# Far token tiles transposed on VectorE from a copy in DRAM, with three orders changed around the attention stage

## The chip, the core and the metric

The kernel runs on one core of a Trainium2 chip. Five engines work side by side, each through its own queue in order: PE (TensorE, matrix products; its weight loads are listed as PEld), DVE (VectorE), ACT (ScalarE), POOL (GpSimd) and SP (SyncE, which here only issues DMA transfers). The metric is the device time of one execution in microseconds (us). Shown are the median of three runs and one further execution that was profiled.

## The reference, cut to what matters

One transformer block over 2048 tokens of width 1024, in float32:

```python
h   = x + A(layernorm(x), wqkv, w_phi, wo)
out = h + relu(layernorm(h) @ w1) @ w2

def A(x, wqkv, w_phi, wo):                     # 32 heads of 32
    q, k, v = heads(x @ wqkv)
    pq, pk = q @ w_phi, k @ w_phi              # a 32x32 matrix for each head
    phi(p) = concat(softmax(p), softmax(-p))
    kv, z = phi(pk).T @ v, sum over tokens of phi(pk)
    o = (phi(pq) @ kv) / (phi(pq) . z + 1e-6)
    return merge(o) @ wo
```

## The kernel before, in words

**Products.** A product is split into three matmuls (`mm3`, lines 182 to 184): an operand is held as a rounded high half and the remaining low half, and high x high, high x low and low x high are summed. ACT makes the high half (a copy), DVE or POOL the low half (a subtraction).

**Steps.** The program is a list of items in a fixed order, and an item is a run of steps; a step is one `mm3` of one weight unit (128x512). In the first part an item is eight steps: one tile of 128 tokens against eight weight units. Items 0 to 31 are keys and values (four column quarters s of eight tiles) for tiles 0 to 7, called near; items 32 to 47 are queries (two halves) for the same tiles; items 48 to 79 and 80 to 95 are the same for tiles 8 to 15, called far. So far tiles are first used at step 384. Output weights follow at item 96, then the two feed-forward products. `when(step, f)` hangs a helper call behind a step; helpers are issued to the engines' queues in that order. What a helper issues runs as early as its data and its queue allow.

**Weight units.** `Units.advance` is called behind every step. It loads raw weight blocks into six buffers and splits them into a ring of ten units: ACT writes the high half (line 125), POOL or DVE the low half (line 129). A group of eight units serves all eight tiles of a quarter, so most of the next eight become writable only while the last item of a quarter runs, one each step, and each is wanted nine steps later. Such a place is called a switch here. Switches lie at steps 64, 128, 192, ... 448, 512 and so on.

**Far tiles.** A near or far tile of x is normalized and turned so that features lie on partitions. For far tiles, `ln_load` and `ln_stats` first read x for its mean and variance (key "s", from step 80 on, 16 steps apart), and `ln_power` (three short POOL instructions, lines 231 to 233) makes the scale. Later x is loaded a second time, normalized on ACT (line 239), transposed by eight PE transposes (`ln_turn`, line 246) into two PSUM banks, and split from there: ACT two copies of 128x512 (line 178), DVE two subtractions of 128x512 (line 179). That is done between steps 321 and 387, tile by tile, eight steps apart.

**Other work of POOL in that stretch.** `t_sum` (line 363, four subtractions of 128x256 at a time) prepares feed-forward weights: a 512 KB load, four subtractions, a 512 KB store, with two buffers in turn. `kv_z` (line 454) adds up key features, `q_fourth` (line 544) makes short products.

**Attention.** Far queries and attention overlap. For each of 32 units u: `at_sums` (POOL, line 595), `at_reduce` (DVE, line 602), `at_cross` (ACT, four 32x32 copies, line 613), `at_den` (POOL, 617 and 618), `at_inverse` (DVE, 621), `at_scale` (POOL, 631), `at_turn` (DVE, a transpose in 32x32 blocks, line 637), and for each pair of units `at_num` (PE, line 650, 32 small matmuls, 16 of each unit) and `at_low` (DVE, 667). Query items need `q_first` (DVE, lines 516 to 521) and `q_third` (DVE, 534 and 535). Six of the output-weight units live in buffers of their own, named `wf`, in a pool opened by `to_far`.

## Time and profile before

| quantity | value |
|---|---|
| median of three runs | 1872.97 us (1872.37 to 1873.45) |
| profiled execution, its own time | 1870.48 us |
| its span, first to last instruction | 1868.7 us |
| mean granted TensorE clock | 0.999 |
| PE busy | 1856.5 us, 99% of the span |
| DVE, ACT, POOL busy | 1063.8, 770.5, 979.0 us |

The span is the time from the first to the last instruction; the execution's own time has 1.8 us more around it. The chain of waits is followed back from the last instruction: at each point it names the work or the wait that was last to end. A timeline row gives start, duration, engine, line, operation and, in brackets, how long the engine sat idle before it and what ended that. Numbers of steps stand nowhere in the trace; they come from the code, by counting the matmuls of line 182, one for each step.

### The profile page before, as it was taken

The page shows a single profiled execution, that of the slowest core. Times are in us where ns is not written, and L with a number is a line of the kernel's source. Part 1 is how long each engine was busy: PE and PEld are TensorE (multiplying, and loading weights), DVE is VectorE, ACT ScalarE, POOL GpSimd, SP SyncE. Part 2 cuts the span into 40 slices and gives each one's busy share as a digit, 9 for nine tenths or more (in the row PEclk, how much of TensorE's full clock was granted, in tenths as well). Part 3 has the DMA queues.
Part 4 walks back from the last instruction along what each step waited for, and adds up shares of the span by engine and source line. Part 5 has one row for each costly group of instructions (what it writes and reads, how often), then busy time and mean ns, then how long its engine had stood idle before and what let it go on. Part 6 is the DMA issues. An engine that isn't in the chain of part 4 may idle for free.

```text
span 1868.7 us, 28840 instructions
## 1 busy us (share of the span) xinstructions
PE 1856.5 (99%) x10064; PEld 1516.3 (81%) x10064; DVE 1063.8 (57%) x1655; ACT 770.5 (41%) x1379; POOL 979.0 (52%) x991
## 2 busy tenths in 40 slices
PE   9999999999999999999999999999999999999999
PEld 7777788888887777888888888888888888888887
DVE  7787678677689878575555653443433333343333
ACT  5322245233333333354455554444444444444442
POOL 4887745888947988343333222222344444444443
PEclk9999999999999999999999999999999999999999
DMA  7988798666575676887888975666677677777765
GB/s 229 286 294 288 231 289 270 190 203 202 178 227 181 223 243 203 280 278 232 247 262 259 324 249 184 193 201 205 225 223 215 216 218 239 238 215 217 216 216 177
DMA packets 333635, 433.04 MB, mean 232 GB/s; under 512 B 28720, under 2 KB 194608, under 8 KB 333488
## 3 DMA queue, kind: packets, MB, share of 16 engines
q1 hardware_dynamic: 299696, 414.41, 70.1%
q10 hardware_dynamic: 33792, 16.78, 3.2%
q8 instruction: 79, 1.29, 0.3%
q14 instruction: 68, 0.56, 0.1%
HBM read 293.21 MB, written 137.89 MB: 231 GB/s over the span
## 4 chain that ended last, share of the span: by engine, by line
PE 93%; DVE 3%; POOL 1%; issue 1%; ACT 0%; DMA 0%; SPq 0%; ACTq 0%; DVEq 0%; POOLq 0%
PE mm L182 24%; PE mm L183 24%; PE mm L184 24%; PE ac L182 4%; PE ac L184 4%; PE ac L183 4%; PE tp L184 2%; PE tp L183 2%; PE tp L182 2%; PE tp L246 1%; PE ac L465 1%; PE ac L650 1%; DVE qsm L534 0%; DVE qe L637 0%; POOL w L129 0%
## 5 line engine op out<-in xcount | busy, mean ns | idle before, releaser
L129 POOL TENSOR_TENSOR w<-raw,w 128x512 fp32r<-128x512 f32 x353 | 469.0, 1331 | 698.3 <-ACT w L125 663.2
L125 ACT ACTIVATE w<-raw 128x512 fp32r<-128x512 f32 x686 | 409.4, 626 | 508.8 <-PE mm L184 232.4
L129 DVE TENSOR_TENSOR w<-raw,w 128x512 fp32r<-128x512 f32 x333 | 271.0, 815 | 511.6 <-ACT w L125 507.6
L182 PE MATMUL mm<-w,xT 128*128 128x512 f32 x768 | 306.0, 398 | 0.0
L183 PE MATMUL mm<-w,xT 128*128 128x512 f32 x768 | 300.2, 391 | 0.4 <-POOL w L401 0.4
L184 PE MATMUL mm<-w,xT 128*128 128x512 f32 x768 | 299.6, 390 | 0.0
L182 PE MATMUL mm<-hT,w 128*128 128x512 f32 x672 | 261.5, 389 | 0.0
L183 PE MATMUL mm<-hT,w 128*128 128x512 f32 x672 | 261.5, 389 | 0.0
L184 PE MATMUL mm<-hT,w 128*128 128x512 f32 x672 | 261.5, 389 | 0.0
L182 PEld LDWEIGHTS mm<-w,xT 128*128 128x128 f32 x768 | 144.4, 188 | 35.2 <-issue 4.1
L184 PEld LDWEIGHTS mm<-w,xT 128*128 128x128 f32 x768 | 144.4, 188 | 30.9
L363 POOL TENSOR_TENSOR b<-b 128x256 f32<-128x256 f32 x176 | 143.6, 816 | 48.0 <-DMA b<-in_w_dram 38.6
L183 PEld LDWEIGHTS mm<-w,xT 128*128 128x128 f32 x768 | 144.6, 188 | 29.2 <-POOL w L401 1.0
L184 PE MATMUL mm<-w 128*128 128x512 f32 x392 | 152.6, 389 | 0.0
L182 PE MATMUL mm<-w 128*128 128x512 f32 x392 | 152.6, 389 | 0.0
L183 PE MATMUL mm<-w 128*128 128x512 f32 x392 | 152.6, 389 | 0.0
L182 PEld LDWEIGHTS mm<-hT,w 128*128 128x128 f32 x672 | 126.2, 188 | 26.4
L183 PEld LDWEIGHTS mm<-hT,w 128*128 128x128 f32 x672 | 126.2, 188 | 26.2
L184 PEld LDWEIGHTS mm<-hT,w 128*128 128x128 f32 x672 | 126.2, 188 | 26.0
L183 PEld LDWEIGHTS mm<-w 128*128 128x128 f32 x392 | 73.6, 188 | 15.3
L184 PEld LDWEIGHTS mm<-w 128*128 128x128 f32 x392 | 73.6, 188 | 15.2
L182 PEld LDWEIGHTS mm<-w 128*128 128x128 f32 x392 | 73.6, 188 | 15.3
(173 smaller groups left out, 3106.0 us busy)
## 6 DMA issues: line engine op xcount, KB each, us to landing
raw<-t SPq DMA_DIRECT2D x224, 256.0 KB, 3.9
raw<-ad SPq DMA_DIRECT2D x196, 256.0 KB, 3.0
raw<-in_w_dram SPq DMA_DIRECT2D x168, 256.0 KB, 3.1
ad<-c SPq DMA_DIRECT2D x112, 256.0 KB, 3.6
b<-in_w_dram SPq DMA_DIRECT2D x44, 512.0 KB, 5.8
t<-b SPq DMA_DIRECT2D x44, 512.0 KB, 5.0
ad<-s SPq DMA_DIRECT2D x84, 256.0 KB, 4.1
ed<-qe ACTq DMA_DIRECT2D x64, 256.0 KB, 4.1
```

The costliest lines, as they stand in the source:

```text
L125: nc.scalar.activation(w[:, 0, :], raw[1], AF.Copy)
L129: eng.tensor_tensor(out=w[:, 1, :], in0=raw[1], in1=w[:, 0, :].bitcast(F32), op=ALU.subtract)
L182: pe.matmul(ps, a_hi, b_hi, start=first, stop=False, skip_group_check=more)
L183: pe.matmul(ps, a_hi, b_lo, start=False, stop=False, skip_group_check=more)
L184: pe.matmul(ps, a_lo, b_hi, start=False, stop=last, skip_group_check=more)
L246: pe.transpose(pt[:, k, :], xn[:, (4 * j + k) * P:(4 * j + k + 1) * P], ident)
L363: pool.tensor_tensor(out=tsum[*u, *out], in0=tsum[*u, *a], in1=tsum[*u, *b], op=ALU.subtract)
L465: pe.matmul(kv_ps[s][g][32 * i:32 * (i + 1), 0:64], vt[:, 32 * h:32 * (h + 1)], phi[:, 64 * h:64 * (h + 1)], start=first, stop=last)
L650: pe.matmul(banks[g][32 * c:32 * (c + 1), 256 * j:256 * (j + 1)], kvL[rows, 2 * q + h // 4, 32 * (h % 4):32 * (h % 4 + 1)], phT_of[u - 1 + ...
```

## The change

**Far tiles.** For tiles 8 to 15, x is read once. Behind its statistics (`early` is now 80 + 26 for each tile) `far_norm` normalizes it on ACT into a second buffer, with features regrouped; `far_keep` stores that buffer to a DRAM tile `xm`, so laid out that tokens and feature groups are exchanged between rows and columns; `far_back` loads it again from step 300 on, 11 steps apart; `far_turn` transposes it in 32x32 blocks on DVE, in place; `far_high` copies the high half on ACT and `far_low` subtracts on POOL, both over 128x1024 elements read with a step of 256 elements innermost. The PE transposes of far tiles, their PSUM copies and subtractions, and the second load of x are gone. The values are the same as before.

**Turn seven.** `at_turn` of unit 7 is issued five steps sooner. **Crossing copies.** For units 8 and up `at_cross` is issued two steps later and `at_den` one step later. **Output-weight buffers.** The pool of `wf` buffers is opened two items sooner, in `to_wo`; three of its six are usable from there and the others from `to_far` on.

```diff
+    xm = {t: dram.tile([P, D], F32, name=f"xm{t}") for t in range(HT, NT)}
...
     def ln_load(key, parts):
-        xin[key] = xlp.tile([P, D], F32, name="xl") if key[0] == "x" and key[1] >= HT and key[1] % 4 > 1 else \
-            lnp.tile([P, D], F32, name="xin")
+        xin[key] = lnp.tile([P, D], F32, name="xin")
...
+    def far_norm(t):
+        sc, src = xst.pop(("s", t)), xin.pop(("s", t))
+        xin["m", t] = y = lnp.tile([P, D], F32, name="xin")
+        act.activation(y.rearrange("p (a c k) -> p c a k", a=4, c=NK), src.rearrange("p (c a k) -> p c a k", a=4, c=NK),
+                       AF.Identity, bias=sc[:, 1:2], scale=sc[:, 0:1])
+
+    def far_keep(t):
+        sp.dma_start(xm[t].rearrange("(a t) (g x) -> (t g) a x", a=4, g=4),
+                     xin.pop(("m", t)).rearrange("p (a x) -> p a x", a=4))
+
+    def far_back(t):
+        xnt["x", t] = y = xlp.tile([P, D], F32, name="xl") if t % 4 > 1 else fp_ln.tile([P, D], F32, name="xn")
+        sp.dma_start(y, xm[t])
+
+    def far_turn(t):
+        v.transpose(xnt["x", t], xnt["x", t])
+
+    def far_view(y):
+        return y.rearrange("p (g c t) -> p c t g", g=4, c=NK)
+
+    def far_high(t):
+        act.activation(xT[t][:, 0].rearrange("p c (t g) -> p c t g", g=4), far_view(xnt["x", t]), AF.Copy)
+
+    def far_low(t):
+        lo, hi = (xT[t][:, s].rearrange("p c (t g) -> p c t g", g=4) for s in (1, 0))
+        pool.tensor_tensor(out=lo, in0=far_view(xnt.pop(("x", t))), in1=f32(hi), op=ALU.subtract)
...
-            early = 80 + 16 * (t - HT)
+            early, late_ = 80 + 26 * (t - HT), 330 + 11 * (t - HT)
             when(early, ln_load, ("s", t), x_part(t))
-            when(early + 18, ln_stats, ("s", t))
-            when(early + 18, xin.pop, ("s", t))
-            when(early + 22, ln_power, ("s", t))
-            load_ = turn - 88 + 8 * (t - HT) if t < HT + 4 else turn - 36
-            stages = (load_, None, None, turn - 8, turn + 1, turn + 1)
+            when(early + 12, ln_stats, ("s", t))
+            when(early + 16, ln_power, ("s", t))
+            when(early + 20, far_norm, t)
+            when(early + 23, far_keep, t)
+            when(late_ - 30, far_back, t)
+            do(n, 0, x_open, t)
+            for step, f in ((0, far_turn), (4, far_high), (7, far_low)):
+                when(late_ + step, f, t)
+            continue
...
+        far = wos.enter_context(tc.tile_pool(name="wofar", bufs=6, side="right", reuse_waits="tile"))
+        for _ in range(3):
+            far.tile([P, 2, 512], F32R, name="wf")
+        W.far = Ring(far, 3, [P, 2, 512], F32R, "wf")
 
     def to_far():
-        far = wos.enter_context(tc.tile_pool(name="wofar", bufs=6, side="right", reuse_waits="tile"))
-        W.far = Ring(far, 6, [P, 2, 512], F32R, "wf")
+        W.far.bufs = 6
...
-                               (14, at_cross), (16, at_den), (18, at_inverse), (20, at_scale), (26, at_turn)):
+                               (14 if u < 8 else 16, at_cross), (16 if u < 8 else 17, at_den), (18, at_inverse),
+                               (20, at_scale), (21 if u == 7 else 26, at_turn)):
```

Three places show how the orders moved. Line numbers past line 199 are higher in the changed kernel. The first is POOL's queue from the switch at step 384 on. `w<-raw,w` is a weight split, `smq` is `q_fourth`, `b` is a part of `t_sum`, `zacc` is `kv_z`. Before:

```order
L129 TENSOR_TENSOR w<-raw,w 128x512 x2
L544 TENSOR_TENSOR smq<-qsm 128x16 x2
L129 TENSOR_TENSOR w<-raw,w 128x512
L544 TENSOR_TENSOR smq<-qsm 128x16 x2
L129 TENSOR_TENSOR w<-raw,w 128x512
L363 TENSOR_TENSOR b<-b 128x256
L544 TENSOR_TENSOR smq<-qsm 128x16 x2
L363 TENSOR_TENSOR b<-b 128x256 x3
L454 TENSOR_TENSOR zacc_360<-zacc_360,kphi 128x512
```

The same stretch of POOL's queue now, where `xT<-xn,xT` and `xT<-xl,xT` are `far_low`:

```order
L129 TENSOR_TENSOR w<-raw,w 128x512 x2
L571 TENSOR_TENSOR smq<-qsm 128x16 x2
L129 TENSOR_TENSOR w<-raw,w 128x512
L281 TENSOR_TENSOR xT<-xn,xT 128x1024
L571 TENSOR_TENSOR smq<-qsm 128x16 x2
L129 TENSOR_TENSOR w<-raw,w 128x512
L281 TENSOR_TENSOR xT<-xn,xT 128x1024
L390 TENSOR_TENSOR b<-b 128x256
L571 TENSOR_TENSOR smq<-qsm 128x16 x2
L390 TENSOR_TENSOR b<-b 128x256 x3
L481 TENSOR_TENSOR zacc_368<-zacc_368,kphi 128x512
L281 TENSOR_TENSOR xT<-xl,xT 128x1024
```

Three of the eight subtractions of `far_low` (tiles 12, 13 and 14) now stand between the splits and sums of this stretch; tile 15's follows a few rows later.

The second place is DVE's queue around unit 7 of attention; `qe<-qe` under STREAM_TRANSPOSE is `at_turn`, `qmx` and `qe<-mm,qmx` are `q_first`, `qtz` is `at_reduce`, `qden` is `at_inverse`. Before:

```order
L602 TENSOR_REDUCE qtz<-ez 128x16
L516 TENSOR_REDUCE qmx<-mm 128x16
L517 TENSOR_REDUCE qmx<-mm 128x16
L520 TENSOR_TENSOR qe<-mm,qmx 128x4x128
L521 TENSOR_TENSOR qe<-qmx,mm 128x4x128
L602 TENSOR_REDUCE qtz<-ez 128x16
L534 TENSOR_REDUCE qsm<-qe 128x4x2x4
L535 RECIPROCAL qsm<-qsm 128x32
L637 STREAM_TRANSPOSE qe<-qe 128x1024
L621 RECIPROCAL qden<-qden 128x32
```

The same stretch of DVE's queue now:

```order
L629 TENSOR_REDUCE qtz<-ez 128x16
L664 STREAM_TRANSPOSE qe<-qe 128x1024
L543 TENSOR_REDUCE qmx<-mm 128x16
L544 TENSOR_REDUCE qmx<-mm 128x16
L547 TENSOR_TENSOR qe<-mm,qmx 128x4x128
L548 TENSOR_TENSOR qe<-qmx,mm 128x4x128
L629 TENSOR_REDUCE qtz<-ez 128x16
L561 TENSOR_REDUCE qsm<-qe 128x4x2x4
L562 RECIPROCAL qsm<-qsm 128x32
L648 RECIPROCAL qden<-qden 128x32
```

The transpose of unit 7 has moved ahead of a `q_first`, a `q_third` and the second `at_reduce` of unit 8; nothing else in this stretch has moved.

The third place is ACT's queue at the output-weight units; `qden<-qtz` is `at_cross`, `oT<-ac` the copy behind `at_num`. Before:

```order
L125 ACTIVATE wf<-raw 128x512
L613 ACTIVATE qden<-qtz 32x32 x4
L125 ACTIVATE wf<-raw 128x512 x2
L613 ACTIVATE qden<-qtz 32x32 x4
L125 ACTIVATE wf<-raw 128x512 x3
```

The same stretch of ACT's queue now:

```order
L125 ACTIVATE wf<-raw 128x512 x2
L640 ACTIVATE qden<-qtz 32x32 x4
L125 ACTIVATE wf<-raw 128x512 x3
L640 ACTIVATE qden<-qtz 32x32 x4
L125 ACTIVATE wf<-raw 128x512
```

Of the six copies for `wf` units, two now stand ahead of the first crossing copies and five ahead of the second, where one and three stood before.

4 lines of the change are left out of this document (2 added, 2 removed).

## The prediction

> **What bounds the kernel now.** I read the page's first part and its chain of waits first, then the waits of PE, then the timeline at each place where PE stood or nearly stood. The share of busy time:
>
> ```profile
> PE 1856.5 (99%) x10064; PEld 1516.3 (81%) x10064; DVE 1063.8 (57%) x1655; ACT 770.5 (41%) x1379; POOL 979.0 (52%) x991
> PE 93%; DVE 3%; POOL 1%; issue 1%; ACT 0%; DMA 0%; SPq 0%; ACTq 0%; DVEq 0%; POOLq 0%
> ```
>
> PE is the bound nearly throughout, so work taken off PE is worth its full time wherever nothing else is late. The chain in order of time holds the far tiles' transposes, first and last of eight groups, 6.34 us apart:
>
> ```profile
> 269.17 0.87 PE tp L246 x8
> ...
> 313.61 0.87 PE tp L246 x8
> ```
>
> What one group costs stands in the timeline of PE:
>
> ```profile
> 268.78 0.39 PE L184 MATMUL mm<-w,xT 128*128 128x512 f32 x1
> 269.01 1.03 PE L246 MATMUL tp<-ident,xn 128*128 128x128 f32 x8
> 269.80 0.48 PE L182 MATMUL mm<-w,xT 128*128 128x512 f32 x1
> 270.12 0.40 PE L183 MATMUL mm<-w,xT 128*128 128x512 f32 x1
> 270.35 0.39 PE L184 MATMUL mm<-w,xT 128*128 128x512 f32 x1
> ```
>
> Matmuls start 0.23 apart (270.12 to 270.35). From 268.78 to 269.80 are 1.02, so 0.79 too much, and the step to 270.12 is 0.09 too long: 0.88 us a group.
>
> The other engines matter at two kinds of place. At a switch a weight split can come too late; in the attention stage DVE and POOL are full. Busy times in three stretches (columns: stretch, length, then PE, PEld, DVE, ACT, POOL, with instruction counts, granted clock, DMA share, GB/s):
>
> ```profile
> 274.00:331.00 57.00, 57.00 (x281) 47.73 (x280) 49.14 (x80) 27.77 (x41) 32.17 (x52) 1.00 0.92 280
> 331.00:377.00 46.00, 46.00 (x319) 37.00 (x318) 27.95 (x59) 12.72 (x25) 37.36 (x38) 1.00 0.63 195
> 592.00:630.00 38.00, 36.09 (x217) 27.32 (x218) 34.03 (x47) 17.54 (x42) 36.32 (x40) 0.96 0.78 246
> ```
>
> POOL is at 56%, 81% and 96% there, DVE at 86% in the first and 90% in the last.
>
> **Removed: 64 PE transposes.** 8 x 0.88 = 7.0 us, all of it on PE with nothing late around it. Gain 7.0.
>
> **The work that replaces them.** Prices by form:
>
> ```profile
> L178 ACT ACTIVATE xT<-tp 128x512 fp32r<-128x512 f32 x32 | 17.9, 595 | 20.5 <-PE tp L246 20.4
> L179 DVE TENSOR_TENSOR xT<-tp,xT 128x512 fp32r<-128x512 f32 x32 | 20.7, 679 | 11.1 <-ACT xT L178 11.1
> L637 DVE STREAM_TRANSPOSE qe<-qe 128x1024 f32<-128x1024 f32 x32 | 39.3, 1227 | 7.5 <-POOL qe L631 5.6 <-POOL qe L626 1.8
> L836 ACT ACTIVATE hT<-hT 128x1024 fp32r<-128x1024 f32 x28 | 29.4, 1052 | 23.0 <-DMA hT<-hs 23.0
> L781 DVE STREAM_TRANSPOSE y<-xin 128x1024 f32<-128x1024 f32 x4 | 8.2, 2040 | 1.2 <-ACT xin L796 1.2
> L129 POOL TENSOR_TENSOR w<-raw,w 128x512 fp32r<-128x512 f32 x353 | 469.0, 1331 | 698.3 <-ACT w L125 663.2 <-DMA ad<-s 12.1 <-DVE c L866 8.3
> ```
>
> ACT gives up two copies a tile (2 x 0.60) for one of 1.05, and its normalization is only moved: less work, hidden. DVE gives up 2 x 0.68 for one transpose of 1.23, in place like line 637: less work; it keeps 86% in a stretch that gets 12% shorter, so it runs at about 95%, still hidden. The second load of x becomes a load of `xm`; the store of `xm` is new, 8 x 512 KB, at 0.92 of the DMA engines' time later but spread over 200 us before that. I take nothing for it. On SP the store waits for the normalization, and `far_back` waits for a buffer that `far_low` frees; queued behind are raw weight blocks and `t_sum` loads, which are loaded well ahead. Bounds 0 and 2 us.
>
> POOL gets something wholly new: eight subtractions of 128x1024. Twice line 129 is 2.66 us. But one operand is read with a large step, and no POOL row has that; DVE's transpose costs 2.04 with a step on one side (line 781) against 1.23 without, 1.66 times. So between 2.66 and 4.4; I take 2.66, since line 129 has the same engine, operands and types, and keep 4.4 for the range.
>
> **Switch at step 384.** These are the fourth sum group and the first split on POOL, and PE's first use of that unit:
>
> ```profile
> 302.76 3.19 POOL L363 TENSOR_TENSOR b<-b 128x256 f32<-128x256 f32 x4 [2.85 <-DMA b<-in_w_dram]
> 306.71 1.28 POOL L129 TENSOR_TENSOR w<-raw,w 128x512 fp32r<-128x512 f32 x1 [0.77 <-ACT w L125]
> ...
> 312.76 0.39 PE L182 MATMUL mm<-w,xT 128*128 128x512 f32 x1
> ```
>
> The split has 4.8 us to spare. The sums before it are paced by their own load and store, not by PE; PE, with seven groups gone, is there 7 x 0.88 = 6.2 sooner, at 306.6. If the sums still end at 305.95, the split ends at 307.2: 0.6 late. `far_low` of tiles 8 to 11 fits into waits like the 2.85 one. One 512 KB load in front of the first sum is gone, which may bring the sums forward by as much. Loss 0.3, between 0 and 4 (with 4.4 us each, four subtractions outgrow their waits by 1.6 each, 6.4 less the slack).
>
> **Switch at step 448.** POOL's idle times between the two switches, and the use that is nearest:
>
> ```profile
> 319.18 1.29 POOL L129 TENSOR_TENSOR w<-raw,w 128x512 fp32r<-128x512 f32 x1 [5.14 <-ACT w L125]
> 321.66 0.73 POOL L363 TENSOR_TENSOR b<-b 128x256 f32<-128x256 f32 x1 [1.19 <-DMA b<-in_w_dram]
> ...
> 345.19 1.30 POOL L454 TENSOR_TENSOR zacc<-zacc,kphi 128x512 f32<-128x512 f32 x1 [0.73 <-DVE kphi L446]
> ...
> 353.12 1.30 POOL L129 TENSOR_TENSOR w<-raw,w 128x512 fp32r<-128x512 f32 x1 [5.12 <-ACT w L125]
> ...
> 358.42 2.99 POOL L129 TENSOR_TENSOR w<-raw,w 128x512 fp32r<-128x512 f32 x2
> ```
> ```profile
> 360.71 0.39 PE L182 MATMUL mm<-w,xT 128*128 128x512 f32 x1
> ```
>
> The fifth unit's split is the first of the two at 358.42; it ends half of 2.99 later, about 0.6 before PE uses it at 360.71. Tile 12's subtraction goes into the 5.14 wait. Tiles 13 to 15 bring 8.0 us against 1.19 + 0.73 + 5.12 = 7.0 of idle time, and PE is another 0.9 sooner: 1.0 + 0.9 - 0.6 = 1.3 late. Loss 1.3, between 0 and 6 (three times 1.74 more).
>
> **Early switches.** The statistics' three POOL instructions now come at other steps. At the switch at step 128 they stand between two splits:
>
> ```profile
> L231 POOL TENSOR_SCALAR sc<-mv 128x1 f32<-128x1 f32 x16 | 3.6, 223 | 35.2 <-DVE mv L224 34.3 <-ACT xn L239 0.7
> L232 POOL TENSOR_TENSOR sc<-sc,half 128x1 f32<-128x1 f32 x16 | 9.1, 568 | 1.3
> L233 POOL TENSOR_SCALAR sc<-mv,sc 128x1 f32<-128x1 f32 x16 | 4.5, 283 | 1.6
> ```
> ```profile
> 118.22 3.00 POOL L129 TENSOR_TENSOR w<-raw,w 128x512 fp32r<-128x512 f32 x2
> ```
> ```profile
> 120.52 0.39 PE L182 MATMUL mm<-w,xT 128*128 128x512 f32 x1
> ```
>
> The first of the two splits ends near 119.8, 0.7 before its use at 120.52; 0.22 + 0.57 + 0.28 = 1.07 more makes it 0.4 late. POOL may also wait there for DVE's statistics (34.3 us in 35.2 of idle time ahead of line 231). Loss 0.6 with the like place at step 256, between 0 and 3.
>
> **Turn seven, crossing copies, buffers.** PE's own waits in the stage are two:
>
> ```profile
> PE ac L650 <- DVE qe L637: 2.8, 2, 2.4
> PE mm L183 <- POOL wf L129: 1.5, 1, 1.5
> ```
>
> and in the timelines of PE, DVE and POOL:
>
> ```profile
> 588.58 0.39 PE L184 MATMUL mm<-w,xT 128*128 128x512 f32 x1
> ...
> 591.94 1.11 PE L650 MATMUL ac<-qe,kvL 64*32 64x256 f32 x16 [2.38 <-DVE qe L637]
> ...
> 595.17 0.39 PE L184 MATMUL mm<-w,xT 128*128 128x512 f32 x1
> ```
> ```profile
> 609.11 0.88 PE L650 MATMUL ac<-qe,kvL 64*32 64x256 f32 x24
> ```
> ```profile
> 607.18 1.23 DVE L637 STREAM_TRANSPOSE qe<-qe 128x1024 f32<-128x1024 f32 x1
> ```
> ```profile
> 627.96 1.71 POOL L129 TENSOR_TENSOR wf<-raw,wf 128x512 fp32r<-128x512 f32 x1
> ```
>
> 588.58 to 595.17 is 6.6 us for 32 small matmuls (1.1 at 591.94 for sixteen includes the slow restart; about 1.0 for all at full pace) and six of 0.23, some 2.6 in all: the wait and the slow clock behind it cost 4.0. With turn seven earlier that stall goes. What is late next is unit 9: its transpose on DVE ends at 608.41, and DVE had hardly been idle for 16 us before, so it comes no sooner; PE, 4.0 early, starts `at_num` at 605.1 and waits there instead, some 3 us. Behind that POOL decides: it is 36.32 of 38.00 us busy up to 630, and the split of the `wf` unit that PE waits for (627.96, to 629.67) has the same POOL work ahead of it in both orders. The crossing copies and the buffers let ACT and DVE work ahead, but the unit is POOL's. So PE leaves this stage no sooner, whatever it gains at unit 7. And the transpose moved ahead of unit 8's reduction makes POOL wait longer there. Loss 0.4, between a gain of 6 (all stalls: 4.0 + 0.4 + 1.5) and a loss of 2.
>
> **Sum.** -7.0 + 0.3 + 1.3 + 0.6 + 0.4 = -4.4 us on the profiled execution's 1870.48, which lies 2.5 under the median of the runs shown. On the median: 1872.97 - 4.4 = 1868.6 us.
>
> **Rivals.** First, the strided subtraction is dear: POOL falls behind and both switches stall. With 4.4 us each the sum is -7.0 + 4 + 6 + 0.6 + 0.4 = +4.0, so 1877 us; it decides above some 3.8 us, where the two switches together cost the 6 us that the rest of the sum gains. For it: line 781 against 637, and POOL's 81% and margins of 0.6. Against it: POOL has never shown such a cost here. [...] Second, nothing is given back before attention: the sums run ahead and fill POOL's gaps; -7.0 + 0.4, so 1866. For it: the removed load. Against: margins of 0.6 at two switches. Third, the attention stalls go as well: -7 - 6, so 1860. Against it: DVE and POOL are full up to 630. Fourth, transfers are late: the stores of `xm` hold up SP and sums in the first 270 us, where the DMA share is up to 0.9; three switches with margins under 0.7 then stall by some 3 each: -7.0 + 1.0 + 10 = +4, so 1877. For it: that share. Against: weight blocks are loaded long ahead.
>
> **How the numbers follow.** No change means here within 0.2%, 3.7 us, about what a measurement of this kernel can tell: from 1869.2 to 1876.7. Forecast (1866.5 to 1871) 0.40, of it 0.28 faster; nothing given back 0.17; attention too 0.07; dear subtraction 0.24, of it 0.15 slower and 0.09 the same; late transfers 0.12, of it 0.10 slower. Faster 0.52, same 0.23, slower 0.25. The range leaves out the third rival's end and the worst of the first: 1863 to 1878.
>
> **What would show it.** No group of line 246 past 60 us but those of the feed-forward part; the group of `far_low` near 2.7 us, not 4; PE waits for POOL splits (`w`, not only `wf`) near the uses at 306, 353 and 120, summing to about 2; the wait of `at_num` on DVE moved from unit 7 to 9 and `wf` still waited for. The prediction is wrong if `far_low` takes over 4 us, if PE shows no wait at unit 9, or if a wait for DMA stands ahead of a weight split.

## The result, and the profile after

The changed kernel takes 1881.9 us (median of six runs, 1878.56 to 1883.17) against 1872.4 for the kernel before: a ratio of 1.0046, 95 % interval 1.0035 to 1.0057. It is slower by 6.5 to 10.7 us, where 4.4 less was forecast. The profiled execution took 1880.32 us, with a span of 1878.5.

The busy times and the chain of waits of the changed kernel:

```profile
PE 1856.6 (99%) x10000; PEld 1512.0 (80%) x10000; DVE 1069.4 (57%) x1647; ACT 778.0 (41%) x1371; POOL 1001.8 (53%) x999
PE 85%; POOL 6%; DMA 4%; DVE 3%; issue 2%; ACT 0%; SPq 0%; ACTq 0%; POOLq 0%; DVEq 0%
```

The first line hides the loss: 64 instructions fewer on PE, yet as much busy time, in part because matmuls lasted longer behind a wait (0.63 us in place of 0.39 behind the first stall below, from 313.2 us on). The second shows it: 10 % of the span is now released by POOL and DMA, where 1 % was before. PE's waits, longest groups (total, times, longest; waits of the first 15 us and of the first weights left out):

```profile
PE mm L183 <- POOL w L129: 6.3, 8, 2.9
PE ac L492 <- DVE kphi L473: 3.8, 1, 3.8
PE mm L183 <- POOL wf L129: 2.7, 1, 2.7
...
PE mm L183 <- DVE w L129: 0.8, 2, 0.5
...
PE ac L677 <- DVE qe L664: 0.2, 1, 0.2
```

Where the time went is read best from PE's lag: the start of each step's first matmul in the changed trace, less its start in the trace before (positive is later). The rows of the experiments are used further down. In rows 9 and 13 to 16 `kv_third` is issued later, by which alone their value at step 448 is 0.9 too low. Each trace is of one execution. The one before took 1870.48 us, 1.9 under its median, so a lag at the end and a difference of medians can lie 2 to 3 us apart.

| kernel | step 310 | 330 | 384 | 420 | 448 | 476 | 758 | 784 | 830 | 2500 |
|---|---|---|---|---|---|---|---|---|---|---|
| changed kernel | +1.2 | +2.7 | -3.7 | +0.2 | +5.8 | +7.4 | +7.4 | +6.7 | +9.3 | +9.4 |
| 1 far tiles alone | +2.0 | +3.2 | -3.1 | +0.8 | +6.3 | +8.1 | +8.1 | +8.3 | +8.2 | +8.2 |
| 2 three orders alone | 0.0 | 0.0 | 0.0 | 0.0 | 0.0 | 0.0 | 0.0 | -0.6 | +2.0 | +2.6 |
| 3 far_low on DVE | +1.7 | +2.5 | -3.9 | +2.9 | +10.5 | +10.5 | +10.6 | +9.9 | +10.9 | +11.1 |
| 4 read straight | +1.5 | +2.8 | -3.6 | -1.7 | +5.0 | +5.7 | +5.7 | +4.4 | +8.2 | +8.2 |
| 5 far_low in four | +1.6 | +3.5 | -2.9 | +1.9 | +3.5 | +12.2 | +12.2 | +11.7 | +15.5 | +16.0 |
| 6 loads early | +1.7 | +1.9 | -4.4 | -3.2 | +2.8 | +4.3 | +4.3 | +3.7 | +6.3 | +7.5 |
| 7 sums later | +1.1 | +3.3 | -3.1 | -3.8 | +1.6 | +3.2 | +3.2 | +2.8 | +5.3 | +5.8 |
| 8 two transposes | -0.2 | -0.2 | -4.7 | -5.4 | -5.4 | -5.4 | -5.4 | -3.4 | -3.3 | -3.3 |
| 9 kv_third later | +2.3 | +4.2 | -2.2 | -3.1 | -3.9 | +3.7 | +3.7 | +5.5 | +5.6 | +5.6 |
| 10 tiles sooner | +1.2 | +3.9 | -2.5 | +2.2 | +2.2 | +7.1 | +7.1 | +10.1 | +9.1 | +9.3 |
| 11 turn seven alone | +0.1 | +0.1 | +0.1 | +0.1 | +0.1 | +0.1 | +0.1 | -0.3 | +0.9 | +0.9 |
| 12 crossing, buffers | +0.4 | +0.4 | +0.4 | +0.4 | +0.4 | +0.4 | +0.4 | +0.7 | +3.0 | +3.7 |
| 13 POOL relieved | +0.9 | +2.9 | -3.4 | -4.4 | -3.8 | -2.8 | -0.7 | +0.9 | +1.0 | +1.4 |
| 14 runs of 32 | +0.9 | +10.6 | +4.2 | +3.3 | +2.3 | +3.3 | +7.0 | +8.6 | +8.6 | +8.6 |
| 15 sums even | +1.7 | +6.0 | -0.3 | -1.3 | -1.2 | +0.6 | +0.6 | +2.5 | +2.6 | +3.1 |
| 16 three sums | +1.8 | +3.9 | -2.4 | -3.3 | -3.3 | -0.9 | -0.9 | +0.6 | +0.7 | +0.7 |

In the first row: 1.2 lost at the early switches, 1.5 at the switch at step 320; then the missing transposes bring 7.2 (eight times 0.8 to 0.9, the last behind step 384); the switch at 384 takes 4.7, the switch at 448 takes 1.6, and between them step 423 takes 5.6, where PE multiplies the key features of the first three far tiles by their values (`kv_third`, line 492). Behind that, the earlier turn seven brings 4.1 and 3.4 and 2.6 are taken back by step 830.

The three stalls between 300 and 370 us, in PE's timeline:

```profile
309.08 0.39 PE L182 MATMUL mm<-w,xT 128*128 128x512 f32 x1
312.40 0.50 PE L183 MATMUL mm<-w,xT 128*128 128x512 f32 x1 [2.94 <-POOL w L129]
...
343.66 0.49 PE L492 MATMUL ac<-kphi,vt 128*32 128x64 f32 x16 [3.83 <-DVE kphi L473]
...
368.14 0.50 PE L183 MATMUL mm<-w,xT 128*128 128x512 f32 x1 [1.22 <-POOL w L129]
```

The first two cost more than their wait, since PE ran at half clock behind them (granted clock 0.50 from 313.17 to 316.55 us, 0.51 from 343.80 to 347.20). The rows of busy time by stretch (the columns are those of the prediction's, granted clock third from the end) show it:

```profile
306.00:318.00 12.00, 9.06 (x33) 6.99 (x32) 9.55 (x13) 6.09 (x8) 11.53 (x13) 0.86 0.86 247
340.00:348.00 8.00, 4.34 (x27) 3.40 (x28) 5.79 (x13) 2.70 (x5) 7.84 (x7) 0.79 0.54 147
```

0.86 over 12 us and 0.79 over 8 us are each 3.4 us at half speed, in which matmuls start 0.43 apart in place of 0.23: some 1.6 us a time.

What made PE wait at the first place is on POOL: the fourth group of `t_sum`, and the split that PE waits for right behind it (the first of two).

```profile
307.48 3.64 POOL L390 TENSOR_TENSOR b<-b 128x256 f32<-128x256 f32 x4 [0.24 <-DMA b<-in_w_dram]
311.08 2.96 POOL L129 TENSOR_TENSOR w<-raw,w 128x512 fp32r<-128x512 f32 x2
```

The sums, which ended at 305.95 before, now end at 311.1. Of these 5.2 us, 4.3 were there already at the first of the five groups between the two switches, which began at 275.35 before and begins at 279.64 now. At the second place the late instruction is on DVE. These are rows of DVE, and then of POOL, ahead of it:

```profile
316.91 1.23 DVE L271 STREAM_TRANSPOSE xn<-xn 128x1024 f32<-128x1024 f32 x1
...
325.49 3.19 DVE L129 TENSOR_TENSOR w<-raw,w 128x512 fp32r<-128x512 f32 x1
...
335.90 1.78 DVE L473 TENSOR_TENSOR kphi<-ke,ksm 128x512 f32<-128x512 f32 x1
```
```profile
316.05 2.96 POOL L281 TENSOR_TENSOR xT<-xn,xT 128x1024 fp32r<-128x1024 f32 x1
...
325.18 2.95 POOL L281 TENSOR_TENSOR xT<-xn,xT 128x1024 fp32r<-128x1024 f32 x1
...
334.20 2.93 POOL L281 TENSOR_TENSOR xT<-xl,xT 128x1024 fp32r<-128x1024 f32 x1
```

A weight split on DVE, 0.68 us in the trace before, took 3.19 and ended 0.55 behind the `far_low` beside it (325.18 + 2.95 = 328.13; 325.49 + 3.19 = 328.68). A product of key features took 1.78 and ended 0.55 behind another. The transpose at 316.91, which reads one operand, ran beside a third `far_low` in its usual 1.23. Nor was every instruction with two operands held: `qe<-mm,qmx` of `q_first` (line 547 at 284.31) ran beside the `far_low` at 282.80 (2.98) in its usual 0.67.

The prices of the new instructions, by form:

```profile
L281 POOL TENSOR_TENSOR xT<-xn,xT 128x1024 fp32r<-128x1024 f32 x4 | 11.9, 2966 | 0.0
L281 POOL TENSOR_TENSOR xT<-xl,xT 128x1024 fp32r<-128x1024 f32 x4 | 11.7, 2926 | 0.0
L277 ACT ACTIVATE xT<-xl 128x1024 fp32r<-128x1024 f32 x4 | 8.4, 2094 | 17.5 <-DVE xl L271 13.2 <-DMA b<-in_w_dram 4.3
L271 DVE STREAM_TRANSPOSE xn<-xn 128x1024 f32<-128x1024 f32 x4 | 4.8, 1210 | 0.0
```

### The profile page after: what moved, and what is told of

It is laid out like the page before. It is cut to its first block, busy times and chain, and to the rows that moved or that the text cites. A ratio compares the mean times of both kernels' runs of the same rounds, so it can differ in the third digit from the quotient of the medians.

```text
span 1878.5 us, 28713 instructions
## 1 busy us (share of the span) xinstructions
PE 1856.6 (99%) x10000; PEld 1512.0 (80%) x10000; DVE 1069.4 (57%) x1647; ACT 778.0 (41%) x1371; POOL 1001.8 (53%) x999
## 4 chain that ended last, share of the span: by engine, by line
PE 85%; POOL 6%; DMA 4%; DVE 3%; issue 2%; ACT 0%; SPq 0%; ACTq 0%; POOLq 0%; DVEq 0%
PE mm L182 21%; PE mm L183 21%; PE mm L184 21%; PE ac L182 4%; PE ac L184 4%; PE ac L183 4%; PE tp L182 2%; PE tp L184 2%; PE tp L183 2%; POOL w L129 1%; POOL b L390 1%; DMA b<-in_w_dram 1%; DMA raw<-in_wv_dram 1%; PE ac L492 1%; PE tp L246 1%
## 5 line engine op out<-in xcount | busy, mean ns | idle before, releaser
L481 POOL TENSOR_TENSOR zacc<-zacc,kphi 128x512 f32<-128x512 f32 x60 | 81.5, 1358 | 11.8 <-DVE kphi L473 11.8
L182 PEld LDWEIGHTS mm<-w 128*128 128x128 f32 x392 | 73.6, 188 | 15.3
L184 PEld LDWEIGHTS mm<-w 128*128 128x128 f32 x392 | 73.6, 188 | 15.3
```

The costliest lines, as they stand in the source:

```text
L182: pe.matmul(ps, a_hi, b_hi, start=first, stop=False, skip_group_check=more)
L184: pe.matmul(ps, a_lo, b_hi, start=False, stop=last, skip_group_check=more)
L481: pool.tensor_tensor(out=zacc[s], in0=zacc[s], in1=phi_of[key], op=ALU.add)
```

## The experiments

Theories: A, POOL's queue is too full with the eight `far_low`; B, the transfers of the exchanged copy make other transfers late; C, DVE and ACT are late by themselves; D, a POOL instruction holds DVE; later E, the key features are late by DVE's work, and F, POOL's total of work up to each switch decides. Times are medians with the ratio to the kernel before and its 95 % interval.

**1. Far tiles alone, with the three orders as before.**

```
-(14 if u < 8 else 16, at_cross), (16 if u < 8 else 17, at_den) ... (21 if u == 7 else 26, at_turn)
+(14, at_cross), (16, at_den) ... (26, at_turn)
 (and the six wf buffers opened in to_far again)
```

> The far tiles as changed, the three orders as before. In the changed kernel PE is 7.35 us behind the kernel before when the attention stage begins and 9.3 behind after it. If that stage is bound by DVE and POOL whatever the three orders are (my theory), this kernel ends 7 to 8 us behind the kernel before (about 1880), with unit 7's wait of some 2.4 us back at at_num. Rival: the earlier turn seven is worth the 4.0 us of the stall that it removes; then this kernel ends 11 to 13 us behind (about 1885). Second rival: the three orders are what costs 2 us in the stage; then 5.5 to 6 us behind.

Measured: 1879.9 us, 1.0038 (1.0025 to 1.0050). PE enters the attention stage 8.1 late and leaves it 8.2 late. By the medians the far tiles cost 7.4 us, and the stage here hands on what it gets. The profile's lags of 8.2 here and 9.4 with the orders differ by 1.2, the medians by 2.0.

**2. The three orders alone, on the kernel before.**

> The kernel before with turn seven, crossing copies and output-weight buffers alone. Theory (PE leaves the stage no sooner): within 1 us of the kernel before, the stall of 4.0 at unit 7 gone and as much given back at unit 9 and the output-weight units. Rival: the stall's 4.0 us are kept, 1868.4. Second rival: the orders cost what the stage lost in the changed kernel, 1.9 us, so 1874.3.

Measured: 1873.4 us, 1.0005 (0.9997 to 1.0014). The stall of 4.0 at unit 7 goes (lag -4.0 at step 768), and by step 784 PE is only 0.6 ahead. It does not wait at unit 9, as the prediction had it, but at four weight units of the output product. The same rows in the changed kernel (PE, the first two of the four and `at_num` of unit 9, ahead of which no wait stands; the 0.2 in the list of waits belongs to unit 11):

```profile
607.11 0.50 PE L183 MATMUL mm<-w,oT 128*128 128x512 f32 x1 [0.48 <-DVE w L129]
...
609.49 0.50 PE L183 MATMUL mm<-w,oT 128*128 128x512 f32 x1 [0.73 <-POOL w L129]
...
615.75 1.15 PE L677 MATMUL ac<-qe,kvL 64*32 64x256 f32 x32
```

So the earlier turn gains nothing: the splits of DVE and POOL come at their own pace.

**11 and 12. Turn seven alone; crossing copies and buffers alone.** These take experiment 2 apart.

> The kernel before with the earlier turn of unit 7 alone. With all three orders PE was 4.0 ahead behind unit 7, 3.4 of it was given back between steps 775 and 783 at splits of output weights, and the wait for a wf split grew from 1.5 to 2.7. Theory (the stage is bound by POOL and DVE, PE's earliness is given back whatever the other orders are): given back by step 810, time within 1.5 us of the kernel before. Rival: the buffers and crossing copies are what makes the splits late; then 2 to 4 us of the gain stay and the time is 1868.5 to 1870.5.

> The kernel before with the later crossing copies and the earlier buffers, without turn seven. Theory: the stall of 4.0 at unit 7 stays, splits and the wf unit are late by up to 1 us more: 1872.5 to 1874. Rival: these two orders cost what turn seven gains, 3 to 5 us, so 1875.5 to 1877.5.

Measured: 1871.5 us, 0.9996 (0.9987 to 1.0005), and 1873.7 us, 1.0005 (0.9996 to 1.0014). Turn seven alone gains 4.0 at unit 7, gives back 3.7 by step 784 and 1.2 behind it, where unit 11's `at_num` now waits 1.6 for its transpose; its wait for `wf` stays 1.5. With the other two orders that wait is 2.7, with slow clock behind it, and PE loses 2.3 to 2.6 there:

```profile
PE mm L183 <- POOL wf L129: 2.7, 1, 2.7
PE ac L650 <- DVE qe L637: 2.4, 1, 2.4
```

Both are too small to be told from no change in the times. In the traces it is the crossing copies and buffers that make the `wf` unit late, which turn seven has no part in.

**3. far_low on DVE.**

```
-        pool.tensor_tensor(out=lo, in0=far_view(xnt.pop(("x", t))), in1=f32(hi), op=ALU.subtract)
+        v.tensor_tensor(out=lo, in0=far_view(xnt.pop(("x", t))), in1=f32(hi), op=ALU.subtract)
```

> The changed kernel with the subtraction of the far tiles on DVE in place of POOL. Theory A (POOL's queue: eight subtractions of 2.95 us stand ahead of weight splits and sums): the stalls at the switches at 384 (3.9 us with the slow clock behind it) and 448 (1.6) go, 5.5 us faster, about 1876.5, unless DVE, whose price for the same form is not known (1.4 us by twice line 179, up to 3), then delays the key features. Theory B (transfers of the exchanged copy make raw blocks and sum loads late): no change at these two places, 1881 to 1883. Theory C (DVE and ACT are what is late in this stretch, as at step 423): the wait there grows from 3.8 us to 5 or more, and the time is at 1883 or above.

Measured: 1881.9 us, 1.0049 (1.0037 to 1.0062). The time is in theory B's range, but neither place is unchanged. The loss at 448 is gone (lag +10.5 at steps 448 and 476); that doesn't show theory A, since PE comes there 4.7 later than in the changed kernel, more than the 1.6 lost there. 384 costs 7.6 (the last 0.8 of the transposes counted) and 423 costs 7.6, with a wait of 5.0, so theory C holds there. DVE has no room for it either:

```profile
L281 DVE TENSOR_TENSOR xT<-xn,xT 128x1024 fp32r<-128x1024 f32 x4 | 10.0, 2498 | 0.0
L281 DVE TENSOR_TENSOR xT<-xl,xT 128x1024 fp32r<-128x1024 f32 x4 | 8.6, 2148 | 0.7 <-ACT xT L277 0.7
```

With `far_low` off POOL the sums ahead of 384 still begin at 279.69 and end at 311.0, and the last four of the five groups wait 1.0 to 2.8 us for their loads, so POOL's own `far_low` alone is not what makes them late. Nor does the move free POOL, because the hold goes the other way too. In the last group (POOL, then DVE) the second subtraction took 2.57 us in place of 0.73 and ended at 309.38, 0.54 behind the DVE instruction:

```profile
306.00 5.00 POOL L390 TENSOR_TENSOR b<-b 128x256 f32<-128x256 f32 x4 [0.98 <-DMA b<-in_w_dram]
```
```profile
306.79 2.05 DVE L281 TENSOR_TENSOR xT<-xl,xT 128x1024 fp32r<-128x1024 f32 x1
```

**4. Reading straight through.**

```
-        return y.rearrange("p (g c t) -> p c t g", g=4, c=NK)
+        return y.rearrange("p (c t g) -> p c t g", g=4, c=NK)
```

> The changed kernel with far_high and far_low reading the turned tile straight through, so that features of the far tiles come out in a wrong order; everything else is the same work. It prices the reading with a step of 256 elements. Expected: the ACT copy falls from 2.09 to about 1.05 us and the POOL subtraction from 2.95 to about 2.66. Theory A: the wait at step 423, ahead of which ACT's copies stand, shrinks by 1 to 2 us, the switches by 0.3 to 0.6, so 1878 to 1880 in all. Theory B: within 1 us of the changed kernel.

Measured: 1880.4 us, 1.0043 (1.0028 to 1.0059), and the prices

```profile
L281 POOL TENSOR_TENSOR xT<-xn,xT 128x1024 fp32r<-128x1024 f32 x4 | 9.6, 2412 | 0.0
...
L277 ACT ACTIVATE xT<-xl 128x1024 fp32r<-128x1024 f32 x4 | 4.2, 1060 | 15.9 <-DVE xl L271 11.5 <-DMA b<-in_w_dram 4.4
```

The step of 256 elements costs ACT a factor of 1.98 (2094 against 1060 ns) and POOL 1.23 (2966 against 2412). In time it matters little: the switch at 384 costs 2.7 in place of 4.7, but step 423 costs 6.7.

**5. far_low in four pieces.**

```
+        for c in range(0, NK, 2):
+            pool.tensor_tensor(out=lo[:, c:c + 2], in0=src[:, c:c + 2], in1=f32(hi[:, c:c + 2]), op=ALU.subtract)
```

> The changed kernel with the subtraction on POOL in four pieces of 128x256, one behind the other. In the changed kernel a weight split on DVE took 3.19 us in place of 0.68 and ended 0.5 behind far_low on POOL, beside which it ran; a product of key features took 1.78. Theory D (DVE is held for as long as one POOL instruction lasts): with pieces of 0.7 to 0.8 us no DVE instruction there lasts over some 1.5 us, the wait at step 423 shrinks by 1.5 to 2.5 us (twice that with the slow clock behind it), 1877 to 1879. Theory A alone (POOL's queue is too full): POOL needs as long or a little longer, 1881 to 1883, with the wait of 3.8 us at step 423 as it was.

Measured: 1885.5 us, 1.0068 (1.0053 to 1.0083): slower than either theory said. The splits on DVE between 250 and 380 us, as least, median and longest duration in ns, in the changed kernel and then here:

```profile
L129 DVE TENSOR_TENSOR w<-raw,w x11: 627/921/3185, 263.1 to 372.7; 128x512 fp32r<-128x512 f32 x11
```
```profile
L129 DVE TENSOR_TENSOR w<-raw,w x11: 626/1041/1586, 263.9 to 377.5; 128x512 fp32r<-128x512 f32 x11
...
L283 POOL TENSOR_TENSOR xT<-xl,xT 128x256 fp32r<-128x256 f32 x16 | 14.3, 931 | 0.0
```

Nothing on DVE is held for over 1.6 us any more, and the wait at 423 falls from 3.8 to 1.4: theory D is right that the length of one POOL instruction decides how long DVE is held. (PE comes 1.7 later to that place, which by itself would take 1.7 off the wait.) But four pieces of 0.92 are 3.7 us in place of 2.95, POOL has 6 us more to do in all, and the switch at 448 costs 8.7.

**6. The first four exchanged tiles loaded early.**

```
-            when(late_ - 30, far_back, t)
+            when((246, 252, 258, 262)[t - HT] if t < HT + 4 else late_ - 30, far_back, t)
```

> The changed kernel with the loads of the first four exchanged tiles at steps 246 to 262 in place of 300 to 333. Theory B (between 250 and 330 us the DMA engines are full, share 0.8 to 1.04, and these loads hold up the stores of query exponentials, the raw blocks and the loads of the sums): the loss of 1.0 to 1.2 us at the switch at step 320 goes, the sums in front of the switch at 384 come 2 us sooner, so its stall of 3.1 falls to about 1, 3 to 5 us in all: 1877 to 1879. Theory A (POOL's own instructions): the switch at 320 gets better by at most 0.3, that at 384 by under 1, so 1880.5 to 1882.

Measured: 1878.8 us, 1.0035 (1.0022 to 1.0048). Lag at the switch at 320: +0.2 in place of +1.5. The switch at 384 costs 2.0 in place of 4.7. Step 423 and the switch at 448 cost as much as they did. That speaks for theory B at the first two places. It does not settle the first: experiments 9 and 10 have the same instructions up to step 320 but for `kv_third` in 9, and lost 1.9 and 2.7 there. The chain of waits that leads to the switch goes, in the changed kernel, through the store of an exchanged tile and that of query exponentials:

```profile
245.03 5.47 DMA xm<-xin
250.53 7.45 DMA ed<-qe
```

In experiments 9 and 13 it goes through a store of `t_sum` (3.25 and 8.91 us) and the load behind it (6.48 and 3.37), in experiment 6 through no transfer of that stretch, and in the kernel before there is no wait. So transfers are late here, but not the same ones in each run, and what decides which stays open. No run takes the stores of `xm` away.

**7. Three sums later.**

```
-        [266, 276, 286, 296, 332, 342, 352, 362, 372] + ... + [650]
+        [266, 276, 286, 296, 338, 358] + ... + [638, 644, 650, 656]
```

> The changed kernel with three of the nine t_sum groups between steps 256 and 384 put at steps 638 to 656, where POOL is idle for most of 30 us; the last group ahead of the switch at 384 is at step 358 in place of 372. Theory A: POOL has 10 us less to do ahead of that switch, the stall of 3.1 us at step 387 and what follows it at 423 (raw blocks loaded late, then 3.8 us) go, 6 to 9 us faster: 1873 to 1876. Theory C (DVE and ACT are late at 423 by themselves): the stall at 384 goes, that at 423 stays at 3 us or more: 1877 to 1879. If the attention stage pays for the later groups, PE falls back behind step 640.

Measured: 1876.0 us, 1.0016 (1.0007 to 1.0026). No stall at 384 (-3.1 to -3.8, where only the last transposes count), and nothing lost for the groups moved behind step 634. Step 423 still costs 5.4 and 448 costs 1.6. Here the raw blocks are in time and the wait is nearly the same (3.7), so the cascade from the switch alone is not what makes `kphi` late; the hold on DVE is still there. POOL, and DVE beside it:

```profile
320.98 2.94 POOL L281 TENSOR_TENSOR xT<-xn,xT 128x1024 fp32r<-128x1024 f32 x1
```
```profile
321.28 3.18 DVE L129 TENSOR_TENSOR w<-raw,w 128x512 fp32r<-128x512 f32 x1
...
325.89 1.19 DVE L271 STREAM_TRANSPOSE xl<-xl 128x1024 f32<-128x1024 f32 x1
...
331.69 1.77 DVE L473 TENSOR_TENSOR kphi<-ke,ksm 128x512 f32<-128x512 f32 x1
...
338.25 1.08 DVE L473 TENSOR_TENSOR kphi<-ke,ksm 128x512 f32<-128x512 f32 x1
```

and the last of these in the kernel before, with PE's use (line 465, the last 16 of 48 for the third tile):

```profile
332.44 0.69 DVE L446 TENSOR_TENSOR kphi<-ke,ksm 128x512 f32<-128x512 f32 x1
```
```profile
338.94 0.88 PE L465 MATMUL ac<-kphi,vt 128*32 128x64 f32 x48
```

The product of the third tile's features ended at 333.1 in the kernel before, 6.3 us ahead of PE's use at 339.4. Here it ends at 339.3, 6.2 later, and PE is there at 335.8, 3.6 sooner: 6.2 + 3.6 - 6.3 = 3.5 of the wait of 3.7. Of the 6.2 us, 2.5 are the hold on the split, 2.3 the two transposes, 0.5 the third tile's exponential, which stands behind a `far_high` on ACT, and 0.3 the products (the second had been held before too, 1.25 us). The last 0.6 are a later start: DVE begins with the first tile at 319.95 (319.40 before) although PE is 3.9 ahead. Ahead of that, on ACT, a query exponential whose input DVE had ready at 313.7 stands behind a `far_high`, which starts when its transpose ends at 314.85:

```profile
314.88 2.10 ACT L277 ACTIVATE xT<-xn 128x1024 fp32r<-128x1024 f32 x1 [3.62 <-DMA ed<-qe]
316.87 1.06 ACT L552 ACTIVATE qe<-qe 128x1024 f32<-128x1024 f32 x1
```

**8. Two transposes for eight, on the kernel before.**

```
-        for k in range(4):
+        for k in range(1 if far else 4):
             pe.transpose(pt[:, k, :], xn[:, (4 * j + k) * P:(4 * j + k + 1) * P], ident)
+        if far:
+            pt = pt[:, 0:1, :].to_broadcast([P, 4, P])
```

> The kernel before with two PE transposes for each far tile in place of eight: the copies and subtractions read the one turned block four times, so the far tiles hold wrong values, and ACT and DVE do the same work. It measures what PE time taken away is worth with no new work elsewhere. 8 x 6/8 x 0.88 = 5.3 us. Theory (PE is the bound wherever nothing is late): 4.5 to 5.3 faster, 1867 to 1868. Rival: PE, 5 us early, waits at the switches at 384 and 448 for splits that other work paces, and no more than 2 us is left: 1870.5 or above. Second rival: the attention stage gives it back.

Measured: 1867.4 us, 0.9972 (0.9961 to 0.9983): 5.2 us faster of 5.3. In the trace PE gains 5.4, waits at no switch, and loses 2.1 behind step 758: 1.5 at unit 7, not by a longer wait (2.4 as before) but by 6.8 us of slow clock behind it in place of 3.4, and 0.5 at step 783. The medians show no such loss. So PE's time is worth its price here, the stage does not swallow earliness, and the loss of the changed kernel is the work put in the transposes' place.

**9. kv_third later**, on the loads of 6 and the sums of 7, with the three orders as before.

```
-        when(8 * (n + (2, 1, 0, 2, 1, 0, 1, 0)[t % HT]) + 22, kv_third, (hf, s, t))
+        when(8 * (n + (2, 1, 0, 2, 1, 0, 1, 0)[t % HT]) + 26, kv_third, (hf, s, t))
```

> Far tiles as changed, with the three orders as before, the early loads of the first four exchanged tiles and the moved sums together, and the products kv_third issued four steps (2.7 us) later. The first two should leave PE about 4.4 us ahead of the kernel before at step 420, with the losses at 423 (3.7 of waiting and 1.5 to 2 of slow clock) and at 453 (1.5) still there. Theory E (the key features are late by DVE work between 320 and 335 us: a split held for 3.2 us beside far_low, a product held for 1.8, two transposes of 1.2, and an exponential behind far_high): four steps of slack take 2.7 of the 3.7 off and all of the slow clock; PE is 2 to 3.5 us ahead at step 448 and 0.5 to 2 at 460, so 1870.5 to 1872.5. Rival: what is late simply moves (the next tiles' features, then the splits), PE no better than 0 at 460: 1873 or above.

Measured: 1876.3 us, 1.0019 (1.0010 to 1.0028). Step 423 costs next to nothing (lag -3.1 ahead of it, -3.0 behind the moved products) where it cost 5.4, and then the switch at 448 costs 6.7: the rival. PE waits there for a split on POOL, which has been busy without a gap since 335 us (PE, then POOL):

```profile
359.75 0.80 PE L183 MATMUL mm<-w,xT 128*128 128x512 f32 x1 [3.97 <-POOL w L129]
```
```profile
358.44 1.26 POOL L129 TENSOR_TENSOR w<-raw,w 128x512 fp32r<-128x512 f32 x1
```

Busy times between 336 and 360 us in the kernel before, here, and in experiment 13:

```profile
336.00:360.00 24.00, 24.00 (x194) 19.39 (x193) 15.01 (x32) 7.41 (x14) 17.60 (x18) 1.00 0.38 116
```
```profile
336.00:360.00 24.00, 19.97 (x131) 15.95 (x130) 18.70 (x39) 8.99 (x18) 23.30 (x22) 0.96 0.48 142
```
```profile
336.00:360.00 24.00, 22.59 (x188) 18.10 (x187) 20.72 (x37) 7.41 (x16) 20.67 (x17) 1.00 0.32 102
```

The fifth number behind the length is POOL: 23.3 of 24 us busy here, 17.6 before. POOL cannot follow a PE that is 3 us ahead.

**10. Tiles sooner**, on the same base without the later `kv_third`: turns at steps 330, 338, 346, 354, 362, 370, 386, 394, and the loads of the last four tiles 22 steps ahead of them in place of 30.

> The same as the run before without its later kv_third, but with the far tiles turned at steps 330, 338, 346, 354, 362, 370, 386 and 394 in place of 330 to 407 with 11 between. Far_low of tile 13 and the transposes of tiles 14 and 15 then stand 10 to 13 steps ahead of where the features of the first far tiles are made. Theory E: no DVE instruction is held beside far_low between 320 and 335 us but by one of them at most, the waits at 423 and at 453 fall to under 1 us each: PE 2.5 to 4.5 ahead at 460, 1868 to 1870. Rival (POOL is too full ahead of the switch at 384): splits there are late by 1 to 3 us and PE is ahead by less than 2 at 460: 1871 or above.

Measured: 1878.4 us, 1.0030 (1.0020 to 1.0041). No loss at 423, as theory E said, but 5.5 at 384 and 4.9 at 448: the rival. The work has moved, POOL's total has not.

**13. POOL relieved**: base of 9, six of the fifteen sums between steps 256 and 448 put elsewhere, the statistics off the switches, and `t_sum`'s buffers dealt out to match (not in the lines below).

```
-    sums_at = [30, 39, 47, 55] + [64 * i + k for i in (1, 2, 3) for k in sixth] + \
-        [266, 276, 286, 296, 332, 342, 352, 362, 372] + [64 * i + k for i in (6, 7, 8, 9) for k in sixth] + [650]
+    sums_at = [30, 39, 47, 55] + [64 * i + k for i in (1, 2) for k in (7, 15, 23, 31, 39, 47, 55)] + \
+        [64 * 3 + k for k in sixth] + [266, 276, 286, 296, 338, 358, 398, 421, 435] + \
+        [64 * i + k for i in (7, 8, 9) for k in sixth] + [635, 642, 648, 653, 657]
-            early, late_ = 80 + 26 * (t - HT), 330 + 11 * (t - HT)
+            early, late_ = (80, 120, 141, 162, 186, 207, 228, 252)[t - HT], 330 + 11 * (t - HT)
```

> Far tiles as changed at the same steps, the three orders as before, early loads of the first four exchanged tiles, kv_third four steps later, and six of the fifteen t_sum groups of steps 256 to 448 put elsewhere (two before step 192, four behind step 634), three of the six between 384 and 448 among them; the statistics' POOL instructions are moved off the switches at 128 and 256. POOL has then about 9 us less between the last two switches, as much as the three far_low there bring. Theory F (POOL's total of work up to each switch decides): no wait of over 1 us at the switches at 384 and 448, the losses of 0.6 and 0.5 at steps 133 and 264 gone, PE 3.5 to 6 ahead of the kernel before at step 460; with 1 to 2 given back in the attention stage 1867.5 to 1870. Rival (the splits follow PE whatever POOL does, or the moved sums cost as much elsewhere): within 2 us of the kernel before, or slower.

Measured: 1873.3 us, 1.0011 (1.0002 to 1.0020). Theory F is right at the switches: no stall at 384 or 448, PE 2.9 ahead from there to step 640, the jumps at steps 133 and 264 gone. Its total is missed, and by the time the rival is right, that the moved sums cost as much elsewhere: 2.0 are lost at 320, 1.4 where `kv_third` now stands, 2.2 at steps 647 to 650, beside the sums put there, and 1.7 in the attention stage.

**14. Runs of 32**: base of 13, the store in four transfers, so that 32 elements lie side by side.

```
-        sp.dma_start(xm[t].rearrange("(a t) (g x) -> (t g) a x", a=4, g=4), ...)
+        for g in range(4):
+            sp.dma_start(xm[t].rearrange("(a t) (g x) -> g t a x", a=4, g=4)[g], y[32 * g:32 * (g + 1)])
-        return y.rearrange("p (g c t) -> p c t g", g=4, c=NK)
+        return y.rearrange("p (g c t) -> p c g t", g=4, c=NK)
```

> The same with the exchanged copy stored by four transfers of 32 rows, so that after the turn 32 elements lie side by side and far_high and far_low read and write runs of 32 in place of single elements 256 apart; the values are the same. Expected: the ACT copy 2.1 to about 1.1 us and far_low 2.95 to about 2.4, as straight reading showed; in time a gain of 0 to 1.5 us over the run before, since POOL saves 0.5 us a tile and the exponentials stand behind a shorter copy. Rival: three more transfers to issue for each tile hold up SP in the first 220 us, 0 to 2 us slower.

Measured: 1879.8 us, 1.0041 (1.0028 to 1.0054). The prices are as expected, 1.06 on ACT and 2.4 on POOL, and from step 330 to 476 it gains 7.3 where experiment 13 gains 5.7. But it loses 9.7 at the switch at 320. The last store on SP's queue:

```profile
247.21 5.08 SPq L265 DMA_DIRECT2D xm<-xin  x4
252.39 1.13 SPq L381 DMA_DIRECT2D b<-in_w_dram  x1
```

Four issues hold SP for 5.1 us, in a stretch with a DMA share of 0.93, where one took 0.58 in experiment 13. They also begin 6.1 later than there. The load behind them, for the next sums, goes out at 252.4 (243.9 in experiment 13), and the sums, the products and query sums behind them, ACT's exponential and at last the splits are late. The rival was right in kind and too small by far.

**15 and 16. Sums lying otherwise**: base of 13 with `kv_third` at + 28, one more sum before step 250, and [638, 644, 650, 656] at the end. In 15 the middle is [262, 276, 290, 338, 358] and [396, 410, 424, 438], in 16 [266, 276, 286, 296, 338, 358] and [398, 421, 435].

> As the run with POOL relieved, but with kv_third two steps later still, and the sums otherwise: one more before step 250, three before and two behind step 300 (in place of four and two), four between 384 and 448 in place of three, and four at steps 638 to 656, where an earlier run showed no loss. Theory F (POOL's total up to a switch) with theory B (the DMA engines decide at step 320): loss at 320 under 1 us, none over 1 at 384 and at 427, at most 1 at 448, none at 647; PE 4 to 5.5 ahead at 640 and, with 2 given back in the attention stage, 2 to 3.5 at the end: 1869 to 1870.5. Rival: three more groups before step 250 make the early switches late, or four are too many before 448: 1871 to 1874.

> The same, but with four sums before step 300 and three between 384 and 448. If POOL before 448 is what is tight, this one is ahead of the run before by 1 to 3 us there; if the DMA engines at 320 are, it is behind by 1 to 2 there. Time 1869 to 1872; rival as before, 1872 to 1875.

Measured: 1873.8 us, 1.0010 (1.0001 to 1.0019), and 1872.1 us, 0.9999 (0.9990 to 1.0008). Neither shows a loss at 647. 1873.8 is in its rival's range, 1872.1 at the border of the two. At step 310 both are 0.9 later than 13: 0.4 each come at steps 133 and 197, where the moved `kv_third` stands, and both lie ahead of the added group's first sum at step 199. The switch at 320 costs 4.3 in 15 and 2.1 in 16, though 15 has one sum less ahead of it: neither theory says that, and it is the place that varies. At 448 the loss is 0.9 in 15 and 1.5 in 16, where PE comes 2.1 sooner. Experiment 13, with the same three groups ahead of 448 as 16, lost nothing there, so POOL's total does not say all about that switch either. A version of the far tiles that loses nothing against the kernel before exists, then, with the three orders as before and six of POOL's 56 sum groups, the statistics, four loads and `kv_third` moved; one that is faster was not found.

## Why the prediction was wrong

By the lags, the terms differ from the forecast by 5.6 (step 423), 4.4 (switch at 384), 1.6 (attention stage), 1.5 (switch at 320), 0.6 (early switches), 0.3 (switch at 448) and -0.2 (transposes). Together that is 13.8 us, all that lies between the forecast of -4.4 and the last lag of +9.4.

**Removed transposes, 7.0.** Right: 7.2 in the trace, and 5.4 of 5.3 in experiment 8.

**Price of far_low, 2.66 of 2.66 to 4.4.** 2.95, near the lower end, so the dear-subtraction rival fell. What each costs DVE beside it was not in the sum.

**"ACT gives up two copies for one of 1.05: less work, hidden."** Mis-sized: 2.1. Line 836 reads straight through, and the step of 256 that was weighed for POOL was not weighed for ACT. Nor was it hidden: in experiment 7 exponentials stand behind two of these copies in the chain that leads to step 423.

**"DVE ... less work; still hidden."** This is the step that failed most. Its own instructions were priced rightly (1.21 against 1.23), but the prediction looked at DVE's share of a stretch and not at a deadline in it. The sum had no term for step 423, where the third tile's features had 6.3 us to spare (333.1 to 339.4), nor for DVE being held by POOL. By experiment 7 the hold on a split (2.5) and two transposes in front of the features (2.3) used most of it up, and PE is 3.6 earlier there. It cost 5.6 us in the changed kernel, and 5.4 with no stall at the switch ahead of it (experiment 7). In the changed kernel itself the features are 10.4 later than before (343.5), since the stall at 384 and a late raw block (ACT waits 2.0 for it) come on top. Experiment 5 shows the hold by the length of the POOL instruction, experiment 9 the missing slack (with four steps more the loss is gone), experiment 10 that it is the place of these tiles that makes it.

**Stores of xm and SP, nothing of 0 to 2.** Too low: 1.5 were lost at the switch at 320, where a store of `xm` stands in the chain of waits. Experiment 6 took 1.3 of it off, but experiments 9 and 10, with the same early loads, lost 1.9 and 2.7 there, so the cause stays open. The sums ahead of 384 came late in part by transfers (2.7 less with four tiles loaded early). That DMA share was 0.92 stood in the prediction; that late stores of query exponentials and late sum loads lead to weight splits did not.

**Switch at 384, 0.3 of 0 to 4.** 4.7, above the upper end: the sums ended 5.2 later, not at the old time. They had begun 4.3 late behind the switch at 320, and in the chain of waits their own stores and loads set the pace from there (5.0, 5.2, 6.5 and 4.2 us), so they did not catch up. Three sums fewer (experiment 7) take the stall away, but that is POOL work and transfers at once. The 3.1 lost to waiting cost 1.6 more in slow clock. The prediction counted slow clock at unit 7, where it was quoted, but not behind its own new stalls.

**Switch at 448, 1.3 of 0 to 6.** 1.6 in the changed kernel: right by luck, since PE came there 5.8 late. With PE 3.0 ahead it is 6.7 (experiment 9), and with three sums less it is nothing or 1.5 (experiments 13 and 16). The slack of 0.6 in the working should be 0.8 (358.42 + 1.50 = 359.92, against 360.71).

**Early switches, 0.6 of 0 to 3.** 1.2 by step 310; 0.6 at step 133 and 0.5 at 264 in the trace, gone when the statistics' steps move, though 0.9 is lost by step 310 there too (experiment 13).

**Attention stage, 0.4, between a gain of 6 and a loss of 2.** The size is inside the bounds: 2.0 lost with all three orders (+7.4 to +9.4). Without them the stage took 0.1 in experiment 1 and 1.7 to 2.2 in 8, 9, 10 and 13, so the orders' own share is not told apart from that, and all of it is measured against one trace before, of an execution 1.9 us under the median. "Moved to unit 9" was wrong: `at_num` does not wait there, and four weight units and the `wf` unit take the 4.1 and more back. "PE leaves this stage no sooner" holds for a gain inside the stage (experiments 2 and 11), and not for one brought into it (experiment 8).

**Rivals.** Late transfers, at 1877, comes nearest in size, and experiment 6 takes 4.0 of the 14.6 us that are lost at the places up to step 476 off by moving four loads. How much of the rest is the stores' doing no run shows. Experiments 9, 10 and 13 show POOL's work as what stands behind the switch at 448: a loss that is taken away ahead of it comes back there until POOL has less to do.

## What to carry to other kernels

Work taken off the busiest engine is worth its time only if the engines that take it over have room at each deadline they serve, not on average: count, for each stretch up to a deadline, the busy time after the change against the length of the stretch, shortened by the gain. A long instruction on POOL can also be a price on DVE's beside it (here a split of 0.68 us took 3.19 beside a subtraction of 2.95, while a transpose kept its 1.23), and a stall on PE can cost 1.6 us more in slow clock (3.4 us at a granted clock of 0.50), or twice that (6.8 us of it in experiment 8), as it did behind most stalls of 2.4 to 4 us here. A change in a row of deadlines is judged by the lag at each of them, since the sum of waits tells neither which is first nor which hides the next.
